# GpSimd in VectorE's share of the softmax exponential: a fraction formed on GpSimd and squared in place on VectorE

## The chip, the core and the metric

The kernel runs on one core of a Trainium2 chip. Four engines do the arithmetic: TensorE (PE; the loading of its weights is listed as PEld), VectorE (DVE), ScalarE (ACT) and GpSimd (POOL). SyncE (SP) issues the DMAs. Each engine works through its own queue in order and waits on semaphores for the others. The metric is the device time of one execution in microseconds (us), as the median of repeated runs. A profile is one execution with every instruction recorded; its span runs from the first to the last instruction.

## The reference

Two layers with the same weights, one after the other. Each is an attention part and a dense part, with a residual and a layer norm in front of both. There are 2048 rows of 448 columns, 16 heads of 28 columns, and 1792 hidden columns.

```
x = A_x
for layer in (0, 1):
    n = layernorm(x)
    q, k, v = split(n @ wqkv)                    # 16 heads of 28
    p = softmax(q @ k.T * 28 ** -0.5)            # 2048 x 2048 for each head
    x = x + concat(p @ v) @ wo
    h = relu(layernorm(x) @ w1 + b1) ** 2
    x = x + h @ w2 + b2
```

## The kernel before, in words

**Units and groups.** The scores are made transposed, in units of 128x512: one head, 512 pairs of key block and query column (two blocks of 128 keys by 256 queries, as a rule). There are 2048 units over both layers. Three units make a group, which has one score tile of three PSUM banks (`sc`, two in rotation). The matmuls of line 916 (`s_stream`) write it. ScalarE takes the exponential of the group in one instruction (line 941, `e_stream`), into a bfloat16 tile `pt` of 128x1536, eleven in rotation. The matmuls of line 1080 (`p_stream`) multiply it with the values; a column of ones among the values gives the sums of the softmax.

**The units that VectorE takes.** ScalarE alone doesn't do all of them. When the planner finds room on VectorE (`apart`), the third unit of a group goes there instead: ScalarE's instruction then covers 1024 columns, and VectorE works on the third bank (`a_unit`, `a_rest`). The scores come already multiplied by log2(e) and 128. VectorE makes the exponential in three instructions:

- `take`, line 995: adds a large constant to the scores in PSUM and writes float32 to SBUF. The constant places the number so that its low 16 bits are the fraction of the exponent of two.
- `square`, line 1008: reads those low half words as int16 (the constant was chosen so that they are centred on zero) and writes a multiple of their square, in float32.
- `close`, line 1016: adds the first result, a constant and the square, and writes int16. These bits, read as bfloat16, are the exponential.

The float32 results lie in a working set: two have tiles of their own (`v_i`, `v_h`), and a third lies in keys that are not needed at the time (`K_sb`), for most of the run. The last result goes into the third part of the group's own `pt` where the unit belongs to the same pass, or else into one of a few spare bfloat16 tiles (`pd`, `h`, parts of `V_sb`).

**What else each engine does.** VectorE also empties PSUM (Q, K, V, the attention output, relu on line 1274, the residual on line 1216), squares the hidden values (line 1281), multiplies by the reciprocal sums (line 1207) and does the layer norm (lines 501, 506, 611). GpSimd does the two small instructions of each layer norm's root (lines 528 and 529) and a few memsets (line 691 among them). TensorE also runs matmuls whose results nobody uses, to keep busy: line 1501, and repeats of line 916.

**What sets the order.** The order on every queue is written ahead of time by a planner in the kernel. It holds streams of operations (`Op`: engine, estimated duration, what it depends on, which buffer it acquires and releases) and always places the operation that can start first; equal starts go by the stream's priority. `apart` decides whether a group gives up its third unit: a working set must be free, and VectorE's planned backlog plus the units in hand (`left`) must lie under a value of the table `PACE`, which has 64 entries along the run. A unit counts 1.80 us in `left`. The buffers are resources (`Res`): `R_pt` for `pt`, `R_v` for the working sets, `R_pd` for the spare tiles. On the chip nothing of this is left but the order of the queues and the semaphores.

```
        c = Op("DVE", 0.69, take, deps=[("s", gi)], acq=sets_of(unit), rel=x)
        h = Op("DVE", 0.684, square, deps=[c])
        o = Op("DVE", 0.683, close, deps=[h, ("e", gi)] if own else [h], acq=None if own else lambda: pd_free(unit), rel=c, sets=("x", gi))
```

## Time and profile before

| what | value |
|---|---|
| median of 3 runs | 849.58 us (849.2 to 850.04) |
| the profiled execution | 848.74 us, of which the span is 847.0 us |
| TensorE busy | 809.2 us, 96% of the span |
| VectorE busy | 793.7 us, 94% |
| ScalarE busy | 826.4 us, 98% |
| GpSimd busy | 41.7 us, 5% |
| mean granted clock of TensorE | 0.994 |
| exponentials on ScalarE (line 941) | 683 instructions: 438 of 1536 columns, 245 of 1024 columns |
| units on VectorE (lines 995, 1008, 1016) | 244 recorded |

How to read the views: a busy time is the time in which at least one instruction of the engine was running; the records of neighbouring instructions on VectorE and ScalarE overlap a little, so the sum of single durations is above the busy time. A group's row gives line, engine, operation, output and inputs with their shapes, the count, the busy time, the mean duration in ns, and the idle time just before these instructions with what ended it. A row of the timeline gives start, duration (both in us), engine, line and operation. The view by windows gives busy time and count of each engine in each stretch. Busy time on TensorE contains the matmuls that nobody uses, and their ends are modelled.

### The profile page before, as it was taken

The page shows a single profiled execution, that of the slowest core. Times are in us where ns is not written, and L with a number is a line of the kernel's source. Part 1 is how long each engine was busy: PE and PEld are TensorE (multiplying, and loading weights), DVE is VectorE, ACT ScalarE, POOL GpSimd, SP SyncE. Part 2 cuts the span into 40 slices and gives each one's busy share as a digit, 9 for nine tenths or more (in the row PEclk, how much of TensorE's full clock was granted, in tenths as well). Part 3 has the DMA queues.
Part 4 walks back from the last instruction along what each step waited for, and adds up shares of the span by engine and source line. Part 5 has one row for each costly group of instructions (what it writes and reads, how often), then busy time and mean ns, then how long its engine had stood idle before and what let it go on. Part 6 is the DMA issues. An engine that isn't in the chain of part 4 may idle for free.

```text
span 847.0 us, 27977 instructions
## 1 busy us (share of the span) xinstructions
PE 809.2 (96%) x12200; PEld 430.6 (51%) x12200; DVE 793.7 (94%) x1563; ACT 826.4 (98%) x699; POOL 41.7 (5%) x94
## 2 busy tenths in 40 slices
PE   8999999999999999999999999998999999999997
PEld 4455555554545545454445554444554454545565
DVE  7999999999999999999899999989999999999965
ACT  8998999999999999999999999999999999999994
POOL 3100000000000010000000000001000000000000
PEclk9999999999999999999999999989999999999999
DMA  9200000000000000000000000011000000000000
GB/s 250 67 2 3 19 24 16 15 16 15 11 6 15 15 16 15 16 3 14 2 3 2 2 2 2 15 30 28 18 24 25 21 21 21 21 13 15 21 9 19
DMA packets 32363, 17.97 MB, mean 21 GB/s; under 512 B 17833, under 2 KB 31787, under 8 KB 32240
## 3 DMA queue, kind: packets, MB, share of 16 engines
q1 hardware_dynamic: 32240, 16.18, 6.9%
q8 instruction: 95, 1.56, 0.8%
q14 instruction: 28, 0.23, 0.1%
HBM read 13.88 MB, written 2.07 MB: 19 GB/s over the span
## 4 chain that ended last, share of the span: by engine, by line
PE 48%; ACT 27%; DVE 15%; issue 7%; DMA 2%; POOL 1%; ACTq 0%; SPq 0%; DVEq 0%
ACT pt L941 27%; PE mt L647 20%; PE sc L916 16%; PE oT L1080 8%; DVE v_i L995 2%; DVE v_h L1008 2%; PE mt L1501 2%; DVE r L1274 1%; DVE pt L1016 1%; DVE K_sb L1008 1%; DVE K_sb L995 1%; DVE st L501 1%; DVE x_sb L1216 1%; DMA rec<-scr 1%; DVE xn L611 1%
## 5 line engine op out<-in xcount | busy, mean ns | idle before, releaser
L941 ACT ACTIVATE pt<-sc 128x1536 bf16<-128x1536 f32 (+1 forms) x683 | 815.7, 1415 | 6.8 <-PE sc L916 6.2
L916 PE MATMUL sc<-Q_sb,K_sb 32*128 32x256 bf16 (+1 forms) x5180 | 306.8, 267 | 27.6 <-ACT pt L941 21.5
L916 PEld LDWEIGHTS <-K_sb 32*128 32x128 bf16 x5180 | 131.6, 92 | 205.9 <-issue 153.1
L1080 PE MATMUL oT<-pt,V_sb 128*32 128x256 bf16 (+1 forms) x4034 | 154.5, 270 | 0.7 <-DVE pt L1016 0.3
L995 DVE TENSOR_SCALAR v_i<-sc 128x512 f32<-128x512 f32 x175 | 119.1, 682 | 6.9 <-PE sc L916 6.1
L647 PE MATMUL mt<-xnT,w 128*128 128x256 bf16 (+1 forms) x888 | 120.3, 271 | 1.0 <-DVE r L1274 0.5
L1008 DVE SCALAR_TENSOR_TENSOR v_h<-v_i 128x512 f32<-128x512 int16 x175 | 117.5, 679 | 0.5
L1080 PEld LDWEIGHTS <-V_sb 128*32 128x32 bf16 x4352 | 90.9, 96 | 50.0 <-issue 46.9
L647 PEld LDWEIGHTS <-w 128*128 128x128 bf16 x896 | 74.3, 98 | 37.7 <-issue 28.9
L1274 DVE TENSOR_SCALAR r<-mt 128x512 bf16<-128x512 f32 x108 | 73.4, 680 | 4.7 <-PE mt L647 4.4
L647 PE MATMUL mt<-w,V_sb 128*128 128x448 bf16 (+1 forms) x288 | 69.3, 348 | 0.0
L995 DVE TENSOR_SCALAR K_sb<-sc 128x512 f32<-128x512 f32 x69 | 47.1, 683 | 3.1 <-PE sc L916 2.4
L528 POOL TENSOR_TENSOR ve<-mv,eps_t 128x2 f32<-128x2 f32 (+1 forms) x33 | 11.5, 348 | 769.3 <-DVE mv L506 769.3
L1008 DVE SCALAR_TENSOR_TENSOR K_sb<-K_sb 128x512 f32<-128x512 int16 x69 | 46.8, 678 | 0.3
L1216 DVE TENSOR_TENSOR x_sb<-x_sb,mt 128x448 bf16<-128x448 bf16 x62 | 37.6, 611 | 7.3 <-PE mt L647 6.8
L1501 PE MATMUL mt<-xn,ident 128*128 128x448 bf16 x128 | 44.1, 357 | 0.3
L1016 DVE SCALAR_TENSOR_TENSOR pt<-v_i,v_h 128x512 int16<-128x512 f32 x64 | 43.0, 672 | 0.3
L1016 DVE SCALAR_TENSOR_TENSOR V_sb<-v_i,v_h 128x512 int16<-128x512 f32 x63 | 42.5, 678 | 0.2
L501 DVE BATCH_NORM_STATS2 st<-x_sb 128x6 f32<-128x448 bf16 x63 | 38.5, 614 | 0.8 <-DMA x_sb<-in_A_x_dram 0.7
L647 PEld LDWEIGHTS <-V_sb 128*128 128x128 bf16 x302 | 24.2, 98 | 25.0 <-issue 11.0
L647 PE MATMUL mt<-wo,oTn 128*128 128x448 bf16 x124 | 31.2, 355 | 0.4 <-DVE r L1274 0.3
L647 PEld LDWEIGHTS <-wk 128*128 128x128 bf16 x256 | 22.2, 97 | 11.4 <-issue 8.3
(133 smaller groups left out, 704.1 us busy)
## 6 DMA issues: line engine op xcount, KB each, us to landing
rec<-scr SPq DMA_DIRECT2D x54, 128.0 KB
x_sb<-in_A_x_dram SPq DMA_DIRECT2D x8, 224.0 KB
out_dram<-x_sb SPq DMA_DIRECT2D x15, 112.0 KB
w<-in_B_w_dram SPq DMA_DIRECT2D x1, 1568.0 KB
w<-in_B_w_dram SPq DMA_DIRECT2D x1, 1344.0 KB
dn<-oT_sb SPq DMA_DIRECT2D x54, 4.0 KB
V_sb<-in_A_wqkv_dram SPq DMA_DIRECT2D x4, 168.0 KB
scr<-dn SPq DMA_DIRECT2D x27, 8.0 KB
```

The source lines that it names most:

```text
L501: nc.vector.bn_stats(out=box["st"][:, :], in_=x_sb[:, t0 + j, :] if src is None else src())
L528: nc.gpsimd.tensor_tensor(out=ve[:, a:b], in0=mv[0][:, a:b, 1], in1=eps_t[:, a:b], op=ALU.add)
L647: nc.tensor.matmul(box["t"][:, c0:c0 + n], lhsT=lhsT() if callable(lhsT) else lhsT, rhs=rhs, start=a, stop=b)
L916: nc.tensor.matmul(dst[k][:, i * nt * P:(i + 1) * nt * P], lhsT=K_sb[l][rows, g, (kb + i) * P:(kb + i + 1) * P], rhs=Q_sb[rows, g, t0 * P: ...
L941: t = nc.scalar.activation(out=pt[:, 0:n], in_=gbuf[gi]["sc"][:, 0:n], func=AF.Exp, scale=float(np.log(2.0)) * 2.0 ** -FRAC)
L995: t = nc.vector.tensor_scalar(out=box["i"], in0=two(src), scalar1=EXP_SHIFT, scalar2=EXP_LOW, op0=ALU.add, op1=ALU.max)
L1008: nc.vector.scalar_tensor_tensor(out=box["h"], in0=box["f"], scalar=EXP_BEND, in1=box["f"], op0=ALU.mult, op1=ALU.mult)
L1016: nc.vector.scalar_tensor_tensor(out=box["two"](pd.bitcast(DT.int16)), in0=box["i"], scalar=EXP_BITS, in1=box["h"], op0=ALU.add, op1=ALU.add)
L1080: nc.tensor.matmul(box["t"][DHP * hh:DHP * hh + DHP, 0:n], lhsT=V_sb[l][:, kb + i, 4 * g + hh, :], rhs=p[:, c0:c0 + n], start=begin and kb ...
L1216: nc.vector.tensor_tensor(out=x_sb[:, tb, lo:hi], in0=x_sb[:, tb, lo:hi], in1=t[:, 0:hi - lo], op=ALU.add)
L1274: nc.vector.tensor_scalar(out=r[:, 0:w], in0=t[:, 0:w], scalar1=0.0, scalar2=None, op0=ALU.max)
L1501: nc.tensor.matmul(t[:, 0:D], lhsT=ident[:, :], rhs=xns[0][:, 0:D], start=True, stop=True)
```

## The change

The second of the three instructions of a VectorE unit is split in two. GpSimd reads the low half words as uint16 (`part`), subtracts the centre, multiplies by the root of the coefficient and writes bfloat16 straight into the tile that will hold the unit's result. VectorE multiplies this tile with itself in place (`bend`, bfloat16). The third instruction (`close`) adds the first result, a constant and the tile, and writes over the tile. The constants are fitted anew, since the centring has moved out of the first instruction.

A working set now holds one float32 tile and not two, so the same memory gives four own sets and two in the keys: six, or four where the keys can't be used. `pt` gets a place in the plan ahead of the exponential (`place`), because GpSimd may write into it first; `close` no longer waits for ScalarE's instruction of the group. The spare tile is acquired by GpSimd's step and not by `close`.

The planner gets a flag `port`: an operation with the flag on VectorE is not started while one with the flag runs on GpSimd, and the other way round. It is set for GpSimd's step and root, and for VectorE's `bend`, `close`, the norm of line 611, the multiplication of line 1207 and the square of line 1281. A unit now counts 1.54 us in `left`. `PACE` has new values; their mean is 2.23 and was 2.38.

```
--- before.py
+++ after.py
@@ -24,11 +24,12 @@
 
 
 FRAC = 7
-EXP_MID = 0.506
+GY = 0.65
+EXP_MID = 0.50773
 EXP_LOW = 128.0 * 128
-EXP_SHIFT = 184.0 * 128 - round(EXP_MID * 2.0 ** 16) / 512
-EXP_BEND = 0.3418455151161652 * 128 / 65536 ** 2
-EXP_BITS = (127.0 - 0.08538929525245402) * 128 - EXP_SHIFT
+EXP_SHIFT = 184.0 * 128
+EXP_BEND = (0.3370821 * 128) ** 0.5 / 65536
+EXP_BITS = (127.0 - 0.085177) * 128 - EXP_SHIFT
 OVER = 0.08
 QUICK = 2
 QUICK3 = 2
@@ -72,7 +73,7 @@
 LEAD = 15
 LAST = 690
 BUSY = 0.995
-PACE = (3.6, 3.6, 3.6, 1.8, 1.8, 1.8, 1.8, 1.8, 0.3, 0.9, 2.2, 2.2, 2.2, 2.6, 3.0, 3.0, 3.0, 3.6, 6.0, 2.2, 2.2, 2.2, 4.5, 2.2, 3.0, 2.6, 2.2, 2.2, 2.6, 2.6, 1.8, 1.8, 2.2, 2.6, 2.6, 1.8, 1.8, 1.8, 2.2, 2.6, 3.0, 6.0, 2.6, 4.5, 1.4, 1.4, 1.4, 1.4, 1.4, 1.4, 1.4, 1.4, 2.2, 2.2, 2.2, 2.2, 2.2, 2.2, 2.2, 2.2, 2.2, 2.2, 2.2, 2.2)
+PACE = (3.6, 2.2, 2.2, 1.8, 1.8, 1.8, 1.8, 3.0, 0.3, 0.9, 2.2, 2.2, 2.2, 1.4, 1.4, 1.4, 1.4, 1.4, 1.4, 2.2, 2.2, 2.2, 2.2, 1.4, 3.0, 3.0, 2.2, 2.2, 2.2, 1.8, 4.5, 4.5, 2.6, 2.6, 3.0, 3.0, 3.0, 3.6, 3.0, 1.4, 3.0, 4.5, 4.5, 4.5, 1.4, 1.4, 0.9, 1.4, 0.3, 1.4, 1.4, 1.4, 2.2, 2.2, 1.8, 1.8, 1.8, 1.8, 2.6, 2.6, 1.8, 1.8, 0.3, 6.0)
 SPAN = 11
 NPT = 11
 NOS = 2
@@ -121,16 +122,16 @@
 
 
 class Op:
-    __slots__ = ("eng", "dur", "fn", "deps", "acq", "rel", "mode", "sets", "start", "end", "res", "turn", "ready", "lat", "need", "got", "more", "room")
-
-    def __init__(self, eng, dur, fn, deps=(), acq=None, rel=None, mode="full", sets=(), lat=0.0, need=1):
+    __slots__ = ("eng", "dur", "fn", "deps", "acq", "rel", "mode", "sets", "start", "end", "res", "turn", "ready", "lat", "need", "got", "more", "room", "port")
+
+    def __init__(self, eng, dur, fn, deps=(), acq=None, rel=None, mode="full", sets=(), lat=0.0, need=1, port=False):
         self.eng = eng if isinstance(eng, tuple) else (eng,)
         self.dur, self.fn, self.deps, self.mode, self.lat = dur, fn, deps, mode, lat
         self.rel = rel if isinstance(rel, list) else ([] if rel is None else [rel])
         self.acq = acq if isinstance(acq, tuple) or callable(acq) else (() if acq is None else (acq,))
         self.sets = sets if isinstance(sets, list) else ([sets] if sets else [])
         self.start = self.end = self.res = self.turn = None
-        self.need, self.got, self.more = need, [], 0.0
+        self.need, self.got, self.more, self.port = need, [], 0.0, port
 
 
 LAT = {"PE": 0.25, "ACT": 0.22, "DVE": 0.10, "POOL": 0.15, "DMA": 2.0, "-": 0.0}
@@ -146,6 +147,7 @@
         self.tok = {}
         self.streams = []
         self.past = {"PE": [], "DVE": []}
+        self.ports = {"POOL": [], "DVE": []}
         self.turns = lambda: False
         self.slack = lambda: SLACK
 
@@ -180,6 +182,10 @@
             s = max(t, self.clock[e])
             if e == "PE" and self.mode != o.mode:
                 s = max(t, self.clock[e] + 0.1)
+            if o.port and e in self.ports:
+                for a, b in self.ports["POOL" if e == "DVE" else "DVE"]:
+                    if a <= s < b:
+                        s = b
             if best is None or s < best[0] - 0.05:
                 best = (s, e)
         return best
@@ -216,6 +222,8 @@
             self.clock[e] = o.end - (OVER if e == "DVE" and o.dur > 0.1 else 0.0)
             if e == "PE":
                 self.mode = o.mode
+            if o.port and e in self.ports:
+                self.ports[e] = [*self.ports[e][-5:], (s, o.end)]
             if e in self.past:
                 self.past[e] = [p for p in self.past[e] if p[1] > s - 40.0] + [(s, max(s, self.clock[e]))]
             for a in o.rel:
@@ -279,7 +287,7 @@
     R_r, R_xt, R_os, R_xn, R_on, R_rec = Res(2), Res(3), Res(NOS), Res(2), Res(2), Res(2)
     R_h = [Res(2), Res(2)]
 
-    R_v = (Res(1), Res(1), Res(1))
+    R_v = tuple(Res(1) for _ in range(6))
 
 
     R_pd = [*[Res(1) for _ in range(5)], Res(NHP), *[Res(1) for _ in range(2)]]
@@ -527,7 +535,7 @@
                 ve = sp.tile([P, 4], DT.float32, name="ve")
                 nc.gpsimd.tensor_tensor(out=ve[:, a:b], in0=mv[0][:, a:b, 1], in1=eps_t[:, a:b], op=ALU.add)
                 nc.gpsimd.tensor_tensor(out=rstd[:, a:b], in0=ve[:, a:b], in1=mhalf[:, a:b], op=ALU.pow)
-            rs = Op("POOL", 0.95, rsqrt, deps=[mv[1][b - 1]], sets=[("rs", t0 + a)] if early else ())
+            rs = Op("POOL", 0.95, rsqrt, deps=[mv[1][b - 1]], sets=[("rs", t0 + a)] if early else (), port=True)
             rss += [rs] * (b - a)
             pl.spawn(EV, iter([rs]))
         box = {}
@@ -611,7 +619,7 @@
                     nc.vector.tensor_scalar(out=xn[:, 0:D], in0=x_sb[:, t0 + j, :],
                                             scalar1=mv[0][:, j, 0:1], scalar2=ln[j],
                                             op0=ALU.subtract, op1=ALU.mult)
-                nm = Op("DVE", 0.39, norm, deps=[rss[j], *([] if x_in is None else [x_in])], sets=[("n", t0, j)] if early else ())
+                nm = Op("DVE", 0.39, norm, deps=[rss[j], *([] if x_in is None else [x_in])], sets=[("n", t0, j)] if early else (), port=True)
                 yield nm
                 xs.append((xn, nm))
 
@@ -801,7 +809,7 @@
         pi, kb, r, hh = unit
         l, qb, *_ = passes[pi]
         if l == 0:
-            return R_v if 2 <= qb <= 6 else R_v[:2]
+            return R_v if 2 <= qb <= 6 else R_v[:4]
         return R_v
 
     def apart(i, now, us, soon=SOON):
@@ -935,15 +943,19 @@
             yield Op("-", 0.0, None, deps=[("s", gi)])
             n = gbuf[gi]["n"] * 512
 
+            def place(e, gi=gi):
+                gbuf[gi]["pt"] = ptp.tile([P, 3 * 512], DT.bfloat16, name="pt")
+            p = gbuf[gi]["p"] = Op("-", 0.0, place, acq=R_pt, need=n // 512 + gbuf[gi].get("in", 0), sets=("p", gi))
+            yield p
+
             def fn(e, gi=gi, n=n):
                 e_now[:] = [e_now[0] + n // 512 + ("x" in gbuf[gi]), gi]
-                pt = gbuf[gi]["pt"] = ptp.tile([P, 3 * 512], DT.bfloat16, name="pt")
+                pt = gbuf[gi]["pt"]
                 t = nc.scalar.activation(out=pt[:, 0:n], in_=gbuf[gi]["sc"][:, 0:n], func=AF.Exp,
                                          scale=float(np.log(2.0)) * 2.0 ** -FRAC)
                 if gbuf[gi].get("x") is gbuf[gi]["s"]:
                     apart_from(gi, t)
-            o = gbuf[gi]["e"] = Op("ACT", n / 1200 + 0.066, fn, deps=[("s", gi)], acq=R_pt, need=n // 512 + gbuf[gi].get("in", 0),
-                                   rel=gbuf[gi]["s"], sets=("e", gi))
+            o = gbuf[gi]["e"] = Op("ACT", n / 1200 + 0.066, fn, deps=[("s", gi), p], rel=gbuf[gi]["s"], sets=("e", gi))
             yield o
             gi += 1
 
@@ -969,19 +981,16 @@
             return V_sb[0][:, 8 + i, :, :].rearrange("p h r -> p (h r)")
         return hp.tile([P, QB], DT.bfloat16, name="h")[:, :]
 
-    v_i = [const.tile([P, 512], DT.float32, name=f"v_i{k}") for k in range(2)]
-    v_h = [const.tile([P, 512], DT.float32, name=f"v_h{k}") for k in range(2)]
+    v_w = [const.tile([P, 512], DT.float32, name=f"v_w{k}") for k in range(4)]
+    two = lambda a: a.rearrange("p (a n) -> p a n", a=2)
 
     def set_of(res, l):
 
         k = R_v.index(res)
-        two = lambda a: a.rearrange("p (a n) -> p a n", a=2)
-        if k < 2:
-            i, h = two(v_i[k][:, :]), two(v_h[k][:, :])
-        else:
-            keys = K_sb[1 - l][:, :, S - 512:S] if l == 0 else K_sb[0][:, :, 0:512]
-            i, h = keys[:, 0:2, :].bitcast(DT.float32), keys[:, 2:4, :].bitcast(DT.float32)
-        return i, h, two
+        if k < 4:
+            return two(v_w[k][:, :])
+        keys = K_sb[1 - l][:, :, S - 512:S] if l == 0 else K_sb[0][:, :, 0:512]
+        return keys[:, 2 * k - 8:2 * k - 6, :].bitcast(DT.float32)
 
     def a_unit(gi, x, src, unit, l):
         yield Op("-", 0.0, None, deps=[("s", gi)])
@@ -989,35 +998,41 @@
 
         def take(e):
             pending[0] -= 1
-            box["i"], box["h"], two = set_of(c.res, l)
-            box["two"] = two
-            box["f"] = box["i"].bitcast(DT.int16).rearrange("p a (n t) -> p a n t", t=2)[:, :, :, 0]
-            t = nc.vector.tensor_scalar(out=box["i"], in0=two(src), scalar1=EXP_SHIFT,
+            box["w"] = set_of(c.res, l)
+            t = nc.vector.tensor_scalar(out=box["w"], in0=two(src), scalar1=EXP_SHIFT,
                                         scalar2=EXP_LOW, op0=ALU.add, op1=ALU.max)
             if x is gbuf[gi]["s"]:
                 apart_from(gi, t)
         c = Op("DVE", 0.69, take, deps=[("s", gi)], acq=sets_of(unit), rel=x)
-        left[0] += 1.80
+        left[0] += 1.54
         yield c
         left[0] -= 0.6
         pl.spawn(lambda now: V_LAST if e_now[1] - gi >= V_AGE or at[0] > ends_at[unit[0]] + V_PAST else V_LATE if now > c.end + V_WAIT else V_PRIO if gi > FIRST else V_FIRST, a_rest(gi, c, box, unit))
 
     def a_rest(gi, c, box, unit):
 
-        def square(e):
-            nc.vector.scalar_tensor_tensor(out=box["h"], in0=box["f"], scalar=EXP_BEND, in1=box["f"],
-                                           op0=ALU.mult, op1=ALU.mult)
-        h = Op("DVE", 0.684, square, deps=[c])
+        own = gbuf[gi]["in"]
+
+        def part(e):
+            pd = gbuf[gi]["pd"] = gbuf[gi]["pt"][:, 1024:1536] if own else pd_of(y)
+            low = box["w"].bitcast(DT.uint16).rearrange("p a (n t) -> p a n t", t=2)[:, :, :, 0]
+            nc.gpsimd.tensor_scalar(out=two(pd), in0=low, scalar1=-EXP_MID * 65536, scalar2=EXP_BEND, op0=ALU.add, op1=ALU.mult)
+        y = Op("POOL", GY, part, deps=[c, ("p", gi)] if own else [c], acq=None if own else lambda: pd_free(unit), port=True)
+        yield y
+
+        def bend(e):
+            pd = gbuf[gi]["pd"]
+            nc.vector.tensor_tensor(out=pd, in0=pd, in1=pd, op=ALU.mult)
+        h = Op("DVE", 0.42, bend, deps=[y], port=True)
         yield h
-        left[0] -= 0.6
+        left[0] -= 0.34
 
         def close(e):
-            pd = gbuf[gi]["pd"] = gbuf[gi]["pt"][:, 1024:1536] if gbuf[gi]["in"] else pd_of(o)
-            nc.vector.scalar_tensor_tensor(out=box["two"](pd.bitcast(DT.int16)), in0=box["i"], scalar=EXP_BITS, in1=box["h"],
+            pd = gbuf[gi]["pd"]
+            nc.vector.scalar_tensor_tensor(out=two(pd.bitcast(DT.int16)), in0=box["w"], scalar=EXP_BITS, in1=two(pd),
                                            op0=ALU.add, op1=ALU.add)
-        own = gbuf[gi]["in"]
-        o = Op("DVE", 0.683, close, deps=[h, ("e", gi)] if own else [h], acq=None if own else lambda: pd_free(unit), rel=c, sets=("x", gi))
-        gbuf[gi]["x"] = o
+        o = Op("DVE", 0.683, close, deps=[h], rel=c, sets=("x", gi), port=True)
+        gbuf[gi]["x"] = y
         yield o
         left[0] -= 0.6
 
@@ -1087,7 +1102,7 @@
                 o = Op("PE", 0.04 + 0.22 * len(now), fn,
                        deps=[*by, *{("V", l, kb + i) for kb in now for i in range(r)}],
                        acq=None if "o" in box else pools_now(),
-                       rel=[gbuf[gi]["e" if w == "x" and gbuf[gi]["in"] else w] for w, gi in by], mode="col")
+                       rel=[gbuf[gi]["p" if w == "e" or gbuf[gi]["in"] else w] for w, gi in by], mode="col")
                 box.setdefault("o", o)
                 yield o
             if last and quick(l, qb, g):
@@ -1206,7 +1221,7 @@
         def mul(e):
             nc.vector.tensor_tensor(out=oTn_of[l, qb][0][:, g:g + 2, 0:n], in0=both,
                                     in1=box["r"][:, :, 0:n], op=ALU.mult)
-        m = Op("DVE", 0.13 + 2 * n / 930, mul, deps=[r, oTn_of[l, qb][1]], rel=pair["own"])
+        m = Op("DVE", 0.13 + 2 * n / 930, mul, deps=[r, oTn_of[l, qb][1]], rel=pair["own"], port=True)
         yield m
         yield Op("DVE", 0.0, None, deps=[m], rel=r)
         norm_end(l, qb, m, 2)
@@ -1282,7 +1297,7 @@
 
             def then(o, b=b, square=square):
                 aside = not s_left and (l, qb) == (1, len(blocks[1]) - 2)
-                b["s"] = Op("ACT" if aside else "DVE", 0.5 if aside else 0.42, square, deps=[o], rel=o)
+                b["s"] = Op("ACT" if aside else "DVE", 0.5 if aside else 0.42, square, deps=[o], rel=o, port=True)
                 return [b["s"]]
             o = yield from mm_tile(
                 [(i * n, n, [(w1[:, dc, fc * P:(fc + 1) * P], xnT[:, dc, 0:n], *([ends[dc // 2]] if split else [])) for dc in range(NDC)])
```

More of the change, by code (lines that the diff above doesn't have):

```diff
@@ L123, with __init__ @@
 class Op:
-    __slots__ = ("eng", "dur", "fn", "deps", "acq", "rel", "mode", "sets", "start", "end", "res", "turn", "ready", "lat", "need", "got", "more", "room")
-    def __init__(self, eng, dur, fn, deps=(), acq=None, rel=None, mode="full", sets=(), lat=0.0, need=1):
+    __slots__ = ("eng", "dur", "fn", "deps", "acq", "rel", "mode", "sets", "start", "end", "res", "turn", "ready", "lat", "need", "got", "more", "room", "port")
+    def __init__(self, eng, dur, fn, deps=(), acq=None, rel=None, mode="full", sets=(), lat=0.0, need=1, port=False):
         self.eng = eng if isinstance(eng, tuple) else (eng,)
@@ L148, in __init__ @@
         self.past = {"PE": [], "DVE": []}
+        self.ports = {"POOL": [], "DVE": []}
         self.turns = lambda: False
@@ L182, in earliest @@
                 s = max(t, self.clock[e] + 0.1)
+            if o.port and e in self.ports:
+                for a, b in self.ports["POOL" if e == "DVE" else "DVE"]:
+                    if a <= s < b:
+                        s = b
             if best is None or s < best[0] - 0.05:
@@ L218, in run @@
                 self.mode = o.mode
+            if o.port and e in self.ports:
+                self.ports[e] = [*self.ports[e][-5:], (s, o.end)]
             if e in self.past:
@@ L280 @@
     R_h = [Res(2), Res(2)]
-    R_v = (Res(1), Res(1), Res(1))
+    R_v = tuple(Res(1) for _ in range(6))
     R_pd = [*[Res(1) for _ in range(5)], Res(NHP), *[Res(1) for _ in range(2)]]
@@ L936, in e_stream, with place @@
             n = gbuf[gi]["n"] * 512
+            def place(e, gi=gi):
+                gbuf[gi]["pt"] = ptp.tile([P, 3 * 512], DT.bfloat16, name="pt")
+            p = gbuf[gi]["p"] = Op("-", 0.0, place, acq=R_pt, need=n // 512 + gbuf[gi].get("in", 0), sets=("p", gi))
+            yield p
             def fn(e, gi=gi, n=n):
                 e_now[:] = [e_now[0] + n // 512 + ("x" in gbuf[gi]), gi]
-                pt = gbuf[gi]["pt"] = ptp.tile([P, 3 * 512], DT.bfloat16, name="pt")
+                pt = gbuf[gi]["pt"]
                 t = nc.scalar.activation(out=pt[:, 0:n], in_=gbuf[gi]["sc"][:, 0:n], func=AF.Exp,
@@ L1208, in mul @@
                                     in1=box["r"][:, :, 0:n], op=ALU.mult)
-        m = Op("DVE", 0.13 + 2 * n / 930, mul, deps=[r, oTn_of[l, qb][1]], rel=pair["own"])
+        m = Op("DVE", 0.13 + 2 * n / 930, mul, deps=[r, oTn_of[l, qb][1]], rel=pair["own"], port=True)
         yield m
```

75 lines of the change are left out of this document (38 added, 37 removed).

## The prediction

> **What bounds the kernel now.** I read the page's engine line first, then the windows, the waits, the groups by form, and last the timeline around GpSimd's few instructions. The engine line and two of its groups, from the page:
>
> ```profile
> PE 809.2 (96%) x12200; PEld 430.6 (51%) x12200; DVE 793.7 (94%) x1563; ACT 826.4 (98%) x699; POOL 41.7 (5%) x94
> ...
> L941 ACT ACTIVATE pt<-sc 128x1536 bf16<-128x1536 f32 (+1 forms) x683 | 815.7, 1415 | 6.8 <-PE sc L916 6.2
> ...
> L1501 PE MATMUL mt<-xn,ident 128*128 128x448 bf16 x128 | 44.1, 357 | 0.3
> ```
>
> Three engines look full. The windows tell them apart (start and end, length, then busy us and count of PE, PEld, DVE, ACT, POOL, then clock, DMA):
>
> ```profile
> 296.40:338.80 42.40, 41.36 (x621) 21.39 (x622) 40.40 (x77) 42.40 (x37) 2.41 (x6) 1.00 0.06 15
> ...
> 677.60:720.00 42.40, 41.11 (x647) 21.18 (x637) 41.50 (x79) 42.40 (x38) 1.57 (x2) 1.00 0.07 21
> ...
> 804.60:847.00 42.40, 37.75 (x791) 25.41 (x789) 24.33 (x67) 31.00 (x28) 1.30 (x3) 1.00 0.05 14
> ```
>
> In the body ScalarE has no idle time at all, VectorE 1 to 2 us in 42; 18 of VectorE's 53 idle us lie in the last window. TensorE's share is padded: line 1501 alone is 44 us of matmuls that nobody uses, and the waits (total us, times, longest) show it waiting for ScalarE:
>
> ```profile
> PE sc L916 <- ACT pt L941: 21.5, 62, 0.9
> ...
> ACT pt L941 <- PE sc L916: 6.2, 11, 2.2
> ...
> DVE xn L611 <- POOL rstd L529: 2.3, 6, 0.6
> ```
>
> So ScalarE's exponentials set the time, and they shrink only when units go to VectorE, which is itself nearly full. The prices of both, by form:
>
> ```profile
> L941 ACT ACTIVATE pt<-sc 128x1536 bf16<-128x1536 f32 x438 | 628.4, 1566 | 4.0 <-PE sc L916 3.6
> L941 ACT ACTIVATE pt<-sc 128x1024 bf16<-128x1024 f32 x245 | 263.6, 1143 | 2.8 <-PE sc L916 2.6
> ...
> L995 DVE TENSOR_SCALAR v_i<-sc 128x512 f32<-128x512 f32 x175 | 119.1, 682 | 6.9 <-PE sc L916 6.1
> L1008 DVE SCALAR_TENSOR_TENSOR v_h<-v_i 128x512 f32<-128x512 int16 x175 | 117.5, 679 | 0.5
> L1016 DVE SCALAR_TENSOR_TENSOR V_sb<-v_i,v_h 128x512 int16<-128x512 f32 x63 | 42.5, 678 | 0.2
> L1281 DVE TENSOR_TENSOR V_sb<-r 128x512 bf16<-128x512 bf16 x67 | 27.7, 413 | 0.3
> L1207 DVE TENSOR_TENSOR oTn<-oT_sb,rec 128x512 bf16<-128x512 f32 x27 | 18.4, 680 | 0.6 <-DMA rec<-scr 0.6
> L611 DVE TENSOR_SCALAR xn<-x_sb,mv,rstd 128x448 bf16<-128x448 bf16 x63 | 23.2, 389 | 3.0 <-POOL rstd L529 2.3 <-PE mt L1501 0.6
> ```
>
> One unit moved makes a 1536 into a 1024: 1566 - 1143 = 0.423 us less of ScalarE, and of the run. The rows of one queue overlap, so I need spacings too. VectorE:
>
> ```profile
> 212.16 0.68 DVE L1008 SCALAR_TENSOR_TENSOR v_h<-v_i 128x512 f32<-128x512 int16 x1
> 212.76 0.41 DVE L1281 TENSOR_TENSOR K_sb<-r 128x512 bf16<-128x512 bf16 x1
> 213.09 0.68 DVE L1274 TENSOR_SCALAR r<-mt 128x512 bf16<-128x512 f32 x1
> ```
>
> A 0.68 us instruction takes 212.76 - 212.16 = 0.60 us of the queue, a 0.41 us one 0.33.
>
> **The change, part by part.** *VectorE's own work.* `square` (679 ns, 0.60 of queue) goes. `bend` is a bfloat16 product in place, nearest row L1281, 413 ns and 0.33 of queue; should it run at L1008's rate, 0.60. I take 0.33, as shape and type are L1281's. `take` and `close` stay at 0.60 each. A unit costs 1.53 in place of 1.80; 244 units save 244 x 0.27 = 65.9 us of VectorE.
>
> *GpSimd's step.* No row has its shape. The nearest:
>
> ```profile
> L331 POOL MEMSET wk<- 128x1024 uint32 x1 | 1.0, 951 | 0.3 <-POOLq L1537 0.3
> ...
> masks.py:199 POOL TENSOR_SCALAR_AFFINE_SELECT ident<-ident 128x128 bf16<-128x128 bf16 x1 | 0.3, 292 | 0.1
> masks.py:197 POOL MEMSET ident<- 128x128 bf16 x1 | 0.2, 204 | 0.0
> ```
>
> The memsets give (951 - 204) / 896 = 0.83 ns a column. From the 292 ns of 128 columns that is 292 + 384 x 0.83 = 0.61 us for 512. Low end, a memset of 512: 204 + 384 x 0.83 = 0.52. High end, all of the 292 ns above a memset's fixed part, 204 - 128 x 0.83 = 98 ns, taken as per column (1.52 ns): 292 + 384 x 1.52 = 0.88. I take 0.61, which adds only columns to a row that reads, computes and writes. Some 265 of them are 162 us on an engine with 5% of work: no bound by itself. The Trainium skill (GPSIMD Engine Reference, section 3.1) speaks against such a step: it gives 769 ns for 512 elements at 1.8 cycles each. By that the step would be 0.77 us, an estimate inside my ends; no run here shows it.
>
> *The collisions.* This decides. The timeline shows GpSimd being held by VectorE:
>
> ```profile
> 118.97 0.55 POOL L528 TENSOR_TENSOR ve<-mv,eps_t 128x2 f32<-128x2 f32 x1 [77.11 <-DVE mv L506]
> 118.72 0.17 DVE L506 BATCH_NORM_AGGREGATE mv<-st 128x2 f32<-128x6 f32 x1
> 118.81 0.66 DVE L1016 SCALAR_TENSOR_TENSOR V_sb<-K_sb 128x512 int16<-128x512 f32 x1
> ...
> 211.75 0.19 POOL L528 TENSOR_TENSOR ve<-mv,eps_t 128x2 f32<-128x2 f32 x1 [16.26 <-DVE mv L506]
> 211.59 0.66 DVE L1274 TENSOR_SCALAR r<-mt 128x512 bf16<-128x512 f32 x1
> ...
> 244.86 1.02 POOL L529 TENSOR_TENSOR rstd<-ve,mhalf 128x2 f32<-128x2 f32 x1
> 244.65 0.68 DVE L1008 SCALAR_TENSOR_TENSOR v_h<-v_i 128x512 f32<-128x512 int16 x1
> 245.25 0.68 DVE L1008 SCALAR_TENSOR_TENSOR K_sb<-K_sb 128x512 f32<-128x512 int16 x1
> ...
> 212.02 0.69 POOL L529 TENSOR_TENSOR rstd<-ve,mhalf 128x2 f32<-128x2 f32 x1
> ```
>
> L528 takes 0.19 us beside L1274, whose input is PSUM, and 0.55 beside L1016, which has two SBUF inputs: it ends at 119.52, about when L1016 does. L529 takes 1.02 in place of 0.69 when it starts inside an L1008. At 245.25 it gets in between two such instructions. The other direction isn't seen: L1008 at 212.16 keeps its 0.68 while L529 runs. But L529 reads two elements, and the new step reads 512. So VectorE's price for a step that is under way when `bend`, `close` or the like is next lies between 0 and the whole step, 0.61 (up to 0.88).
>
> I call this stall s, per unit. Chance alone would give: instructions of that kind fill about 265 x 0.93 + 27.7 + 23.2 + 18.4 = 316 us of 840, 37% (0.93 is `bend` and `close`; the three figures are the rows of L1281, L611 and L1207), and of a 0.61 us step about half is left when the next instruction comes: 0.37 x 0.3 = 0.11. The planner moves some away, and a step that came late makes `bend` wait on its semaphore instead. I take s = 0.10, near the chance value. What stands behind a waiting `bend` on VectorE's queue is everything there: the next `take`, which frees a score bank for line 916, and relu and the copies from PSUM; behind line 916 waits ScalarE.
>
> *Working sets.* Six in place of three let a unit's `take` run before the unit ahead is closed, so that GpSimd's step has cover: the next `take` or relu on VectorE. Without this cover `bend` would wait the whole step plus the hand-over (0.08 us from L506's end at 118.89 to L528's start at 118.97), 0.7 us a unit; that is the upper end of s.
>
> *Small edits, each at nothing.* The `pt` reserved earlier: ScalarE waits 6.8 us in all, and for scores; if all eleven tiles were taken, ScalarE would idle. The spare tile is held longer, by the step and its hand-over, which can stop GpSimd's queue. On that queue the layer norm's two instructions and the memsets now stand behind the steps, up to 0.61 plus a hold each; L611 waits for them 2.3 us now, six times; if each of the six paid 0.6 more, VectorE would lose 3.6 us and the run under 1. No DMA moves, and SP's queue is untouched.
>
> *The sum.* VectorE gains 65.9 - 244 s; n more units take 1.53 + s each. I keep its share of the run at 0.937, so its budget falls by 0.937 x 0.423 = 0.396 us for each unit that shortens the run: n = (65.9 - 244 s) / (1.926 + s). With s = 0.10: 41.5 / 2.03 = 20 units, 20.5 x 0.423 = 8.7 us. The profiled execution, 848.74 us (span 847.0 and 1.7 around it), becomes 840.0; it lies 0.84 under the median of the runs, so 841 for a median.
>
> **The rivals.** *Cover is complete* (s near 0): 65.9 / 1.926 = 34 units, 14.5 us, 835. For it: VectorE's rows never stretch now. Against: no read as long as the new one exists now.
>
> *The step blocks VectorE* (slower). Place: VectorE's queue, at `bend` and `close` right behind GpSimd's step. It decides from s = 65.9 / 244 = 0.27 us, where nothing is gained. At s = 0.5, most of one step for every unit, VectorE lacks 56 us; if the plan gives units back, 56 / 2.43 = 23 units, 9.8 us, 859. If the plan doesn't know of the stalls, its units stay, and VectorE's lateness lands on the score banks instead: the same order of time or more. For it: 0.93 us of such instructions and 0.61 of a step in every 3.2 us (847 / 265) between units leave little room for a miss. The Trainium skill (SBUF — State Buffer, Who interferes with whom) says the pair of ports is locked by whichever starts first, for the whole instruction. By that rule this rival is the mechanism at work; the trace agrees where GpSimd is held (0.55 against 0.19), and differs or can't tell where VectorE would be (0.68 kept at 212.16).
>
> *The count doesn't rise.* `PACE` is lower (2.23 against 2.38), though a unit counts 1.54 and not 1.80 in it. VectorE would only idle more: 849 to 850. Against: 2.23 / 1.54 = 1.45 units of backlog, more than 2.38 / 1.80 = 1.32.
>
> **How the numbers follow.** Forecast (s from 0.03 to 0.2, 837 to 846): 0.45. Complete cover (below 837, down to 831 if six sets also fill some of the body's idle time): 0.12. No rise, or s near 0.27 (846 to 852): 0.11. Blocking (above 852, to 870): 0.32. About 0.2% (1.7 us) can be told from no change: 847.9 to 851.3. Faster is 0.45 + 0.12 + 0.02 of the third, 0.59; same 0.06; slower the rest, 0.35. With cases of both signs I let the range run from 832 to 862; the forecast's own is 836 to 847.
>
> **What would show it.** `bend` at 413 ns and the step near 0.61 us on GpSimd, about 265 times: the prices hold. About 265 units, and some 20 more exponentials of 1024 columns in place of 1536: the gain was used. `close` or `bend` with means well over 0.68 and 0.41, or a wait of VectorE for GpSimd of more than 26 us in the list of waits: s is larger than I took. Idle ScalarE in the body with TensorE waiting for VectorE: the blocking rival. I am wrong if the step takes above 0.9 us, or if its lock stops VectorE at every unit.

## The result and the profile after

The changed kernel takes 846.35 us (median of 6 runs, 845.38 to 848.54) where the kernel before takes 849.24 (6 runs, 848.55 to 850.04). The ratio is 0.9968 (95% interval 0.9954 to 0.9983): faster by 0.3%, where I had forecast 1.0%. The profiled execution took 845.42 us, its span is 843.6.

The engine line of the page of the changed kernel, and one row of its windows (start and end, length, then busy us and count of PE, PEld, DVE, ACT, POOL, then clock, DMA share and GB/s):

```profile
PE 806.6 (96%) x12255; PEld 428.6 (51%) x12255; DVE 783.8 (93%) x1610; ACT 821.3 (97%) x700; POOL 225.3 (27%) x354
```

```profile
379.60:421.80 42.20, 39.57 (x602) 20.68 (x603) 41.41 (x88) 41.17 (x35) 12.61 (x18) 1.00 0.03 8
```

In the body ScalarE is no longer full everywhere: in this window it is idle for 1.0 us, while VectorE does 41.4 of 42.2. The groups by form of the three engines concerned:

```profile
L954 ACT ACTIVATE pt<-sc 128x1536 bf16<-128x1536 f32 x422 | 607.8, 1541 | 4.7 <-PE sc L924 4.0 <-PE oT L1095 0.3
L954 ACT ACTIVATE pt<-sc 128x1024 bf16<-128x1024 f32 x261 | 278.7, 1113 | 4.4 <-PE sc L924 4.0 <-ACT pt L954 0.3
```

```profile
L1002 DVE TENSOR_SCALAR v_w<-sc 128x512 f32<-128x512 f32 x187 | 127.4, 683 | 10.7 <-PE sc L924 9.9
L1032 DVE SCALAR_TENSOR_TENSOR V_sb<-v_w,V_sb 128x512 int16<-128x512 f32 x74 | 51.5, 698 | 0.1
L1025 DVE TENSOR_TENSOR pt<-pt 128x512 bf16<-128x512 bf16 x99 | 45.1, 468 | 0.7 <-POOL pt L1019 0.7
L1025 DVE TENSOR_TENSOR V_sb<-V_sb 128x512 bf16<-128x512 bf16 x89 | 41.4, 474 | 2.5 <-POOL V_sb L1019 2.5
L619 DVE TENSOR_SCALAR xn<-x_sb,mv,rstd 128x448 bf16<-128x448 bf16 x63 | 26.0, 437 | 2.6 <-POOL rstd L537 2.6
L1222 DVE TENSOR_TENSOR oTn<-oT_sb,rec 128x512 bf16<-128x512 f32 x27 | 21.8, 806 | 1.3 <-DMA rec<-scr 1.3
```

```profile
L1019 POOL TENSOR_SCALAR V_sb<-v_w x74: 617/617/1110, 31.6 to 784.4; 128x512 bf16<-128x512 uint16 x74
```

(The last row is from the view of line 1019: minimum, median and maximum in ns.) The step takes 617 ns when nothing disturbs it. `bend` (L1025) has its 0.41 us as its usual value, but means of 0.47; `close` (L1032), the norm (L619) and the product (L1222) are longer too. 16 more units left ScalarE: 261 exponentials of 1024 columns where there were 245.

**Where the time went.** Back to back, ScalarE's exponentials start 1.330 us apart (1536 columns) and 0.903 us (1024 columns): the shortest spacings in the trace. The first starts at 10.7 us and the last ends 14.4 us before the end, in both kernels. What lies between, less all exponentials at their shortest spacing, is ScalarE's waiting. I use this sum for every run below, with the two ends of each run's own trace (25.0 to 26.8 us together; 29.9 with the old table, where the last exponential ends 19.2 us before the end):

| run | exponentials of 1536 and 1024 columns | ScalarE's waiting, us | span, us |
|---|---|---|---|
| before | 438 and 245 | 18.1 | 847.0 |
| changed | 422 and 261 | 21.6 | 843.6 |

(Before: 847.0 - 25.1 - 438 x 1.330 - 245 x 0.903 = 18.1.) Sixteen units give 16 x 0.427 = 6.8 us; the waiting takes 3.5 of it back. So two things are to be explained: the units that are missing, and the waiting.

**The collisions.** From the timeline of the changed kernel, GpSimd's step and VectorE's queue around it, twice:

```profile
58.10 0.62 POOL L1019 TENSOR_SCALAR V_sb<-v_w 128x512 bf16<-128x512 uint16 x1 [3.20 <-DVE v_w L1002]
...
57.93 0.42 DVE L1123 TENSOR_TENSOR K_sb<-oT,K_sb 128x256 f32<-128x256 f32 x1
58.26 0.73 DVE L1025 TENSOR_TENSOR V_sb<-V_sb 128x512 bf16<-128x512 bf16 x1
...
104.60 0.99 POOL L1019 TENSOR_SCALAR V_sb<-v_w 128x512 bf16<-128x512 uint16 x1 [1.03 <-DVE v_w L1002]
...
104.43 0.68 DVE L1032 SCALAR_TENSOR_TENSOR V_sb<-v_w,V_sb 128x512 int16<-128x512 f32 x1
105.03 0.83 DVE L1025 TENSOR_TENSOR V_sb<-V_sb 128x512 bf16<-128x512 bf16 x1
```

At 58.26 a `bend` starts while the step of another unit runs: 0.73 us in place of 0.42, ending 0.27 us after the step. At 104.60 it is the step that comes in the middle of a `close`: it takes 0.99, which is 0.37 more than usual, so by these times it begins its work about when the `close` ends; the `bend` behind that boundary then takes 0.83. So both directions exist: this is the stall that the trace of before could not show. Of VectorE's instructions of these kinds 82 are more than 60 ns over their usual time, by 28.2 us together (L1025 39 times, 14.4 us; L1032 18, 5.5; L619 10, 3.0; L1222 10, 3.4; L1296 5, 1.9). That is 0.11 us a unit.

### The profile page after: what moved, and what is told of

Read it like the earlier page. It is cut to its first block, busy times and chain, and to the rows that moved or that the text cites. A ratio compares the mean times of both kernels' runs of the same rounds, so it can differ in the third digit from the quotient of the medians.

```text
span 843.6 us, 28341 instructions
## 1 busy us (share of the span) xinstructions
PE 806.6 (96%) x12255; PEld 428.6 (51%) x12255; DVE 783.8 (93%) x1610; ACT 821.3 (97%) x700; POOL 225.3 (27%) x354
## 4 chain that ended last, share of the span: by engine, by line
PE 44%; DVE 27%; ACT 22%; issue 5%; DMA 1%; POOL 0%; SPq 0%; ACTq 0%; DVEq 0%
ACT pt L954 22%; PE mt L655 18%; PE sc L924 15%; PE oT L1095 8%; DVE v_w L1002 3%; DVE pt L1032 2%; DVE r L1289 2%; DVE V_sb L1032 2%; DVE K_sb L1002 2%; DVE pt L1025 2%; DVE V_sb L1025 1%; PE mt L1516 1%; DVE xn L619 1%; DVE oTn L1222 1%; DVE Q_sb L674 1%
## 5 line engine op out<-in xcount | busy, mean ns | idle before, releaser
L924 PE MATMUL sc<-Q_sb,K_sb 32*128 32x256 bf16 (+1 forms) x5258 | 308.6, 267 | 22.3 <-ACT pt L954 17.1
L924 PEld LDWEIGHTS <-K_sb 32*128 32x128 bf16 x5258 | 131.1, 92 | 202.5 <-issue 157.5
L1095 PE MATMUL oT<-pt,V_sb 128*32 128x256 bf16 (+1 forms) x4008 | 154.2, 270 | 1.2 <-DVE pt L1032 0.7
L1002 DVE TENSOR_SCALAR v_w<-sc 128x512 f32<-128x512 f32 x187 | 127.4, 683 | 10.7 <-PE sc L924 9.9
L1095 PEld LDWEIGHTS <-V_sb 128*32 128x32 bf16 x4352 | 91.4, 96 | 50.9 <-issue 47.7
L1019 POOL TENSOR_SCALAR V_sb<-v_w 128x512 bf16<-128x512 uint16 x74 | 54.2, 733 | 131.1 <-DVE v_w L1002 130.3
L1019 POOL TENSOR_SCALAR pt<-v_w 128x512 bf16<-128x512 uint16 x69 | 46.2, 670 | 114.0 <-DVE v_w L1002 91.4
L1032 DVE SCALAR_TENSOR_TENSOR V_sb<-v_w,V_sb 128x512 int16<-128x512 f32 x74 | 51.5, 698 | 0.1
L1032 DVE SCALAR_TENSOR_TENSOR pt<-v_w,pt 128x512 int16<-128x512 f32 x69 | 47.7, 694 | 0.1
L1025 DVE TENSOR_TENSOR pt<-pt 128x512 bf16<-128x512 bf16 x99 | 45.1, 468 | 0.7 <-POOL pt L1019 0.7
L1025 DVE TENSOR_TENSOR V_sb<-V_sb 128x512 bf16<-128x512 bf16 x89 | 41.4, 474 | 2.5 <-POOL V_sb L1019 2.5
L1019 POOL TENSOR_SCALAR pt<-K_sb 128x512 bf16<-128x512 uint16 x30 | 21.6, 719 | 71.9 <-DVE K_sb L1002 51.5
L1516 PE MATMUL mt<-xn,ident 128*128 128x448 bf16 x105 | 36.5, 364 | 0.9 <-DVE oT_sb L1123 0.3
```

What stands on the lines that cost most here:

```text
L924: nc.tensor.matmul(dst[k][:, i * nt * P:(i + 1) * nt * P], lhsT=K_sb[l][rows, g, (kb + i) * P:(kb + i + 1) * P], rhs=Q_sb[rows, g, t0 * P: ...
L1002: t = nc.vector.tensor_scalar(out=box["w"], in0=two(src), scalar1=EXP_SHIFT, scalar2=EXP_LOW, op0=ALU.add, op1=ALU.max)
L1019: nc.gpsimd.tensor_scalar(out=two(pd), in0=low, scalar1=-EXP_MID * 65536, scalar2=EXP_BEND, op0=ALU.add, op1=ALU.mult)
L1025: nc.vector.tensor_tensor(out=pd, in0=pd, in1=pd, op=ALU.mult)
L1032: nc.vector.scalar_tensor_tensor(out=two(pd.bitcast(DT.int16)), in0=box["w"], scalar=EXP_BITS, in1=two(pd), op0=ALU.add, op1=ALU.add)
L1095: nc.tensor.matmul(box["t"][DHP * hh:DHP * hh + DHP, 0:n], lhsT=V_sb[l][:, kb + i, 4 * g + hh, :], rhs=p[:, c0:c0 + n], start=begin and kb ...
```

## The experiments

**A step that hardly reads.** Same order on every queue; only GpSimd's step differs.

```
-            nc.gpsimd.tensor_scalar(out=two(pd), in0=low, ...)                          # cut short
+            nc.gpsimd.tensor_scalar(out=two(pd)[:, :, 0:8], in0=low[:, :, 0:8], ...)    # cut short
+            nc.gpsimd.memset(two(pd)[:, :, 8:256], 0.0)
```

> The changed kernel with the same order on every queue, but GpSimd's step reads and computes only 16 of its 512 columns; the other 496 are set to zero by a memset, so the exponentials of VectorE's units are wrong and only the time is of use. Duration on GpSimd stays near the 0.62 us of the step. Theory A (the collisions that the order doesn't foresee make VectorE late, and ScalarE then waits for scores): the long instances of bend, close, the norm, the square and the product on VectorE, which add some 30 us there, go, and the run falls by 2 to 3.5 us, to 843 to 844. Theory B (the order itself leaves ScalarE waiting, and VectorE's stalls fall into its idle time): the long instances go all the same, and the run stays within 1 us of the changed kernel's 846.

Measured: 843.55 us (5 runs), 0.9930 of before (0.9916 to 0.9945). `bend` in the groups by form of this run, and GpSimd's two instructions:

```profile
L1026 DVE TENSOR_TENSOR pt<-pt 128x512 bf16<-128x512 bf16 x99 | 40.0, 415 | 1.3 <-POOL pt L1020 1.2
...
L1020 POOL MEMSET pt<- 128x496 bf16 x99 | 51.4, 519 | 4.0
L1019 POOL TENSOR_SCALAR V_sb<-v_w 128x16 bf16<-128x16 uint16 x74 | 22.7, 306 | 122.0 <-DVE v_w L1002 119.7 <-DVE dn L1204 1.0
```

GpSimd is at work for at least as long (0.25 to 0.31 us and 0.52), but for most of that time it only writes, and `bend` is back at 415 ns. VectorE's stretch by the count above is 2.1 us in place of 28.2, all of it in the norm. ScalarE's waiting is 18.2 us, what it was before the change. (The exponentials of this profile begin 1.6 us later, at 12.25 us; the mean granted clock of its first 13 us is 0.87, where it is 1.00 in the profile of the changed kernel. This is no part of the waiting.) With this order the collisions cost 2.8 us, as theory A said.

Since the order is the same, single places can be compared. In the changed kernel a step stretches a `close`; TensorE's product (L1095) waits for that `close`; the scores (L924) stand behind the product on TensorE's queue; and ScalarE waits for the scores:

```profile
382.08 0.72 POOL L1019 TENSOR_SCALAR pd<-v_w 128x512 bf16<-128x512 uint16 x1 [2.16 <-DVE v_w L1002]
382.25 1.09 DVE L1032 SCALAR_TENSOR_TENSOR pt<-v_w,pt 128x512 int16<-128x512 f32 x1
383.39 0.60 PE L1095 MATMUL oT<-pt,V_sb 128*32 128x256 bf16 x13 [0.34 <-DVE pt L1032]
383.92 0.60 PE L924 MATMUL sc<-Q_sb,K_sb 32*128 32x256 bf16 x6
384.62 1.45 ACT L954 ACTIVATE pt<-sc 128x1536 bf16<-128x1536 f32 x1 [0.65 <-PE sc L924]
```

With the small read the same `close` takes its usual time, and the spacing of the same pair of exponentials is 0.28 us over the shortest in place of 0.78:

```profile
381.93 0.68 DVE L1033 SCALAR_TENSOR_TENSOR pt<-v_w,pt 128x512 int16<-128x512 f32 x1
```

**The step twice.**

```
+            nc.gpsimd.tensor_scalar(out=two(pd), in0=low, ...)     # once more, the same; cut short
```

> The changed kernel, GpSimd's step issued twice in a row with the same input and output: the result is unchanged, the order elsewhere too. GpSimd holds the port for about 1.2 us a unit in place of 0.62. Theory A: VectorE's stretched time about doubles, to 60 us or more, bend waits for GpSimd in many units besides, and the run rises by more than 8 us. Theory B: VectorE's 60 us of idle time take most of it, and the run rises by 0 to 5 us.

Measured: 893.56 us (4 runs), 1.0519 of before (1.0503 to 1.0535), 47 us over the changed kernel. The waits of this run:

```profile
ACT pt L954 <- PE sc L924: 35.0, 68, 4.3
...
DVE V_sb L1026 <- POOL V_sb L1020: 18.3, 22, 1.4
DVE pt L1026 <- POOL pt L1020: 13.0, 20, 1.2
```

ScalarE's waiting is 68.9 us. VectorE's stretch is 62.5 us, as theory A said, and it waits 41 us for GpSimd besides, so the 47 us are both together. VectorE's idle time, 60 us in the changed kernel, gave no shelter; 18 of it lie in the last 42 us of the run, where no unit is left, and a late `bend` can use none of that.

**No flags in the planner.**

```
-        self.need, self.got, self.more, self.port = need, [], 0.0, port
+        self.need, self.got, self.more, self.port = need, [], 0.0, False
```

and a `PACE` searched anew.

> The changed kernel without the planner's port flags, its table PACE searched anew against the planner's own end time (838.2 us there, against 838.1 for the changed kernel), 274 units on VectorE in place of 260. Theory A: with nothing keeping them apart the steps meet bend and close more often, 40 to 60 us of stretch in place of 30, and the run is 3 to 8 us above the changed kernel, 849 to 854. Theory B: the extra stalls vanish in idle time and 14 more units count, 840 to 846.

Measured: 863.66 us (4 runs), 1.0171 of before (1.0152 to 1.0189). Both theories missed it, and by the wrong quantity: the stretch on VectorE is 33 us, counted as above, little more than the 28 with flags. The engine line of this run:

```profile
PE 809.1 (94%) x12045; PEld 424.0 (49%) x12045; DVE 807.2 (94%) x1653; ACT 821.5 (95%) x699; POOL 230.8 (27%) x368
```

The trace has 275 units in place of 261 and VectorE 807.2 us of work, 94% of the span, the share of the kernel before. ScalarE's waiting is 44.9 us. A poorer plan is not the cause: the planner's end is 838.2 us here and 838.1 for the changed kernel, yet the spans are 860.9 and 843.6, which is 22.7 and 5.5 over the plan. Nor are absent flags by themselves: the run without flags and without collisions, further below, is 3.9 over its plan (838.2 against 834.3). So it is the collisions, in a plan that doesn't leave room for them. My reading, which no run isolates, is that such a plan gives VectorE more units than it can do, so that its lateness adds up, and that the flags do less to prevent collisions than to leave time for them.

**The old table.** The changed kernel with the `PACE` of the kernel before.

```
-PACE = (3.6, 2.2, 2.2, 1.8, ...)
+PACE = (3.6, 3.6, 3.6, 1.8, ...)
```

> The changed kernel with the table PACE of the kernel before, all else as changed: 267 units on VectorE. By the planner's own times this order leaves ScalarE waiting 21.6 us between exponentials, where the changed kernel's order leaves 5.4. Both theories: clearly slower, 855 to 865, though 7 more units leave ScalarE; if the run came out near 846 the order's own waits would mean nothing on the chip.

Measured: 862.67 us (4 runs), 1.0158 of before (1.0141 to 1.0175). It has 268 units and 35.7 us of ScalarE's waiting, and 4.8 us more lie behind its last exponential. So the table decides over far more time than the change moves, and a comparison of two kernels with a table fitted to one only says little of the design. The next four runs therefore have tables searched by the same method: small random changes, kept when the planner's own end time fell.

**The kernel before, with a searched table.** Only `PACE` differs.

> The kernel before with nothing changed but the table PACE, searched against the planner's own time: planned end 841.4 us in place of 843.6, 241 units in place of 244, ScalarE's planned waits 0.8 us in place of 4.3. If the plan's waits count on the chip: 846 to 847.5, as fast as the changed kernel, so that a table alone is worth as much as the change. If not: 849 to 850.5, as 3 units go back to ScalarE.

Measured: 847.45 us (11 runs, 846.89 to 847.58), 0.9981 of before (0.9972 to 0.9990).

**The changed kernel, with a searched table.** Only `PACE` differs.

> The changed kernel with nothing but the table PACE searched in the same way: planned end 834.7 us in place of 838.1, 257 units in place of 260, ScalarE's planned waits 0.7 us in place of 5.4. If the plan's waits count: 841 to 844, faster than both kernels. If collisions undo what the plan says: 846 or more.

Measured: 841.16 us (6 runs, 840.50 to 845.48), 0.9918 of before (0.9898 to 0.9938). It is the fastest of the real kernels. The exponentials of the two runs, first the kernel before, then the changed one:

```profile
L941 ACT ACTIVATE pt<-sc 128x1536 bf16<-128x1536 f32 x441 | 631.5, 1576 | 3.5 <-PE sc L916 3.3
L941 ACT ACTIVATE pt<-sc 128x1024 bf16<-128x1024 f32 x242 | 260.4, 1152 | 0.9 <-PE sc L916 0.8
```

```profile
L954 ACT ACTIVATE pt<-sc 128x1536 bf16<-128x1536 f32 x425 | 611.9, 1554 | 1.6 <-PE sc L924 1.1
L954 ACT ACTIVATE pt<-sc 128x1024 bf16<-128x1024 f32 x258 | 277.0, 1134 | 1.7 <-PE sc L924 1.2 <-ACT pt L954 0.2
```

ScalarE's waiting is 15.5 us in the one (span 845.6) and 15.0 in the other (span 838.7). With the waiting alike, the 16 units between them give 845.6 - 838.7 = 6.9 us, and 16 x 0.427 is 6.8. (That the two agree follows from how the waiting is reckoned. What the pair shows is that 16 more units can leave ScalarE without more waiting.) The stretch on VectorE is still 27 us in the second. By the medians, 847.45 and 841.16, the design is worth 0.7% of the run, and what the changed kernel showed of it depends on its table.

Part of these 0.7% goes with TensorE's granted clock, which differs between executions. Between 520 and 580 us its mean is 0.89 in the profile of the kernel before and 0.94 in that of the changed one, and ScalarE's waiting there is 4.2 and 2.6 us. Executions with like means over the whole span lie closer together: 845.1 and 839.7 us of span at 0.994, 845.6 at 0.991 and 842.5 at 0.990. That is 0.6% and 0.4%, with one execution on each side.

**Three working sets.**

```
-    R_v = tuple(Res(1) for _ in range(6))
+    R_v = tuple(Res(1) for _ in range(3))
```

(and two in place of four at the ends of a layer), with a searched table.

> The changed kernel with three working sets in place of six (two at the ends of a layer in place of four), PACE searched anew: planned end 838.0 us, 259 units. If the cover that I gave the six sets is needed, bend waits for GpSimd in many units and the run is above 850. If not, 844 to 847, as the changed kernel.

Measured: 844.51 us (4 runs), 0.9946 of before (0.9931 to 0.9961). `bend` needs no cover from six sets. The 3 us to the searched table with six sets can't be put down to the sets: the search with three sets ended at 838.0 us of the planner's time, the one with six at 834.7, but both stopped in what may be local minima.

**Nothing collides, and nothing is kept apart.** The step that hardly reads, no flags, a searched table.

> As the run with the small read (GpSimd reads 16 columns of 512, zeros elsewhere, so VectorE's exponentials are wrong and only the time is of use), and the planner's port flags are off as well, with PACE searched anew against the planner's own time: nothing collides and nothing is kept apart. 271 units on VectorE, planned end 834.3 us. Theory A (the shared port is what keeps the rest of the gain, part in collisions and part in the plan's avoiding them): 837 to 840, the rival of complete cover. Theory B (ScalarE's waits come from elsewhere): no faster than the small read with the old order, 843 to 845.

Measured: 840.05 us (4 runs), 0.9912 of before (0.9884 to 0.9940): 272 units, ScalarE's waiting 19.8 us. That is at the edge of what theory A gave, and by the medians not below the 841.16 of the real kernel by more than the two intervals allow. At a like granted clock it is: its two executions at 0.990 have spans of 838.2 and 838.3 us, the real kernel's one has 842.5. Even without collisions and flags no execution came under 839.96 us, so the kernel doesn't come to the 835 of my rival.

**The step that hardly reads, with the searched table's order.**

> The changed kernel with the searched table (841.2 us) and its order, but GpSimd reads 16 of 512 columns and sets the rest to zero, so VectorE's exponentials are wrong and only the time is of use. If a collision costs the run about the same wherever it stands (2.8 us in the changed kernel's own order): 838 to 839. If an order with little planned waiting of ScalarE absorbs the collisions: 840 to 841.5, and what the change's own table lost was its order's lack of room, which the collisions used up.

Measured: 842.69 us (5 runs), 0.9930 of before (0.9917 to 0.9944); the intervals overlap with those of the real step under the same order (0.9898 to 0.9938). ScalarE's waiting is 17.6 us against 15.0, as if taking the collisions away gained nothing here. But the two profiles differ in TensorE's granted clock. The windows from 520 to 580 us, first the real step, then the small read:

```profile
520.00:580.00 60.00, 56.98 (x876) 28.77 (x874) 57.59 (x118) 58.62 (x53) 21.87 (x27) 0.94 0.10 25
```

```profile
520.00:580.00 60.00, 57.30 (x817) 27.82 (x818) 51.17 (x108) 54.69 (x48) 22.85 (x48) 0.83 0.09 21
```

In this stretch, at clocks of 0.94 and 0.83, ScalarE's waiting is 2.6 us with the real step and 7.2 with the small read; in the rest of the run it is 11.9 and 10.0. (These are the spacings alone; the sums above also have the last exponential's record in them, which is 0.4 to 0.5 us longer than its spacing.) So outside the stretch taking the collisions away gains 1.9 us. The executions say the same. All five with the small read have mean clocks of 0.988 to 0.990 and spans of 840.7 to 842.1 us; the two of the real step at such clocks have 842.5 and 843.6, and its other four, at 0.994 to 0.996, have 838.7 to 839.7. At a like clock the collisions thus cost some 2 us with this table too, where they cost 2.8 under the change's own. The medians hide it. It rests on the five executions against two. Whether the lower clock comes with the small read or by chance stays open.

## Why the prediction was wrong

The direction and most prices held. The size failed in the last step of the sum: a unit's saving didn't reach the run in full, since ScalarE came to wait longer, and fewer units were moved.

- **What bounds the kernel: right.** Units that leave ScalarE shorten the run by 0.427 us each at equal waiting (0.423 forecast). No run tested TensorE's share by itself.
- **VectorE's own work: right.** `bend` takes 0.41 us where nothing disturbs it. VectorE's busy time adds up: before, 793.7 less 244 units of 1.80 leaves 354.5 us of other work; with 260 recorded units of 1.53 and 28 us of stretch this gives 780.5, and the profile says 783.8.
- **GpSimd's step: right.** 0.617 us, forecast 0.61. The Trainium skill's 769 ns (GPSIMD Engine Reference, section 3.1), which it gives for a tight unrolled loop, doesn't fit this instruction; the measured time decides.
- **The collisions: right in size on VectorE.** 0.11 us a unit in stretch and 0.01 in waits for GpSimd (2.5 and 0.7 us among them), against s = 0.10. The working by chance comes out as well, 82 / 260 = 0.32 stalls a unit of 0.34 us each against 0.37 and 0.3; in part this may be luck, since the plan was to move some of them away. The lock that the Trainium skill states (SBUF — State Buffer, Who interferes with whom) holds in both directions here, VectorE's too. The price isn't the whole step: `bend` is at most 834 ns, 417 over its usual, while the step is 617.
- **The count: 16 and not 20.** The formula with the measured s, (65.9 - 244 x 0.12) / (1.926 + 0.12), gives 18. I had kept VectorE's share of the run at 0.937; the order uses 0.929. That the flags leave holes on the queues may be why (without them the share is 0.938), but no run shows it by itself. Against the 20.5 of the sum 4.5 units are lacking, 1.9 us at the forecast's price.
- **The failed step: "that shortens the run" for every unit.** I took ScalarE's waiting as it was, which is 18.1 us by the spacings. It rose to 21.6, which ate half of what the units gave. The row that I quoted for its smallness, ScalarE waiting 6.2 us for scores, became 8.0:

```profile
ACT pt L954 <- PE sc L924: 8.0, 12, 3.1
```

I had named ScalarE as the last in line behind a waiting `bend`, by way of a late `take`, but the sum charged s to VectorE's time alone, as units that don't fit, and put nothing on ScalarE. The runs show that price: in the changed kernel's own order, taking the collisions away brings the waiting back to 18.2 and the run down by 2.8 us. The path in the one place followed above is a late `close`, TensorE's product that waits for it, and the scores behind the product. Of the 3.5 us, 2.3 lie between 380 and 464 us, where ScalarE waits 3.2 us against 0.9 before and 1.3 with the small read. The granted clock is not behind this: between 520 and 580 us, where it falls, its mean is 0.91 in the profiles before and after. With the 4.5 units that are lacking (1.9 us) this makes up the gap between the 8.7 us of the sum and the 3.3 between the two profiled executions. The order has its own part in the waiting: another table comes to 15.0 us with 27 us of stretch in place. Which of the 82 stalls reach ScalarE, beyond the one followed, stays open.

- **The rivals.** Complete cover (835) fell: 840.05 with nothing in the way. Blocking as the main effect (859) did not come in the changed kernel, but a plan without the flags shows it at 863.66, and a step of twice the length at 893.56. "The count doesn't rise" fell, although `PACE` is lower.

## What to carry to other kernels

Where a planner writes the order ahead, price a change with its table fitted for both versions: here the table alone moved the changed kernel from 846 to 841 or 863, more than the change itself. Work moved to GpSimd beside VectorE must be counted in the plan as time on both queues while it reads: 28 us of stalls cost 2.8 us where the plan kept the two apart, and with 33 us of stalls in a plan that did not, the run was 17 us above the changed kernel. A saving on the second-fullest engine reaches the run only through the waiting of the fullest one: look at the latter's spacing, not at its busy share. And before a difference of 2 us is put down to an edit, compare the granted clock of the executions: here it hid the gain of one run and enlarged that of another.

## What the runs showed of the hardware

- VectorE and GpSimd hold each other up in both directions when GpSimd reads 512 columns and VectorE's instruction has two SBUF inputs (or is the norm of line 619, bfloat16 from SBUF to SBUF). GpSimd gets in at the boundary between two such instructions of VectorE, even when they stand back to back. A memset of 496 columns on GpSimd, 0.52 us, left `bend` at its 415 ns.
- GpSimd's step costs 0.617 us for 512 columns, and 0.205 for 16: 0.83 us more for each 1000 columns, the slope of its memsets.
- In some executions TensorE's clock is lower for the first microseconds, in others not. This window is from the run of the step that hardly reads, with 0.87 as its clock; in the changed kernel the same stretch has 1.00:

```profile
0.00:13.00 13.00, 9.77 (x61) 5.73 (x62) 7.48 (x31) 8.99 (x12) 5.83 (x16) 0.87 0.81 230
```

The first exponential starts at 12.2 us there and at 10.7 otherwise. This 1.6 us is as large as some of the differences compared here, and the medians contain it or not by chance; in the sums of ScalarE's waiting it is left out, since they begin at the first exponential.
